# A fourth silu buffer and an earlier last product in the fast-product units of a fused attention and feed-forward kernel

## The chip, the cores and the metric

The kernel runs on one core of a Trainium2 chip. Its time is the device time of one execution in microseconds (us). The core has five instruction streams: TensorE (PE in the profile, PEld for its weight loads), VectorE (DVE), ScalarE (ACT), GpSimd (POOL) and SyncE (SP), which here only starts transfers. Each stream runs its own instructions in order and waits for the others through semaphores.

## The reference

A decaying linear attention over blocks of 64 positions (4 batches, 8 heads, 768 positions, head size 64) is followed by a gated feed-forward block on the 3072 tokens:

```python
for b in range(nb):                       # blocks of 64
    intra = einsum('bhic,bhjc->bhij', qb, kb) * Dmask
    intra = einsum('bhij,bhjd->bhid', intra, vb)
    inter = einsum('bhid,bhde->bhie', qb * lam_pow, kv_state)
    out[:, :, sl] = intra + inter
    kv_state = lam_block * kv_state + einsum('bhsd,bhse->bhde', kb * rev_pow, vb)
x = out.transpose(0, 2, 1, 3).reshape(3072, 512)
g = x @ w_gate                            # 512 x 1536
val = x @ w_val                           # 512 x 1536
return (g / (1 + exp(-g)) * val) @ w_out  # 1536 x 512
```

## The kernel before

The attention runs in twelve groups (each one batch and 256 positions). Two groups make a token tile of 512 columns, `xt`; there are six tiles, 0 to 5. While the feed-forward block of one tile runs on PE, the attention of a later tile is slipped between its products. The order of all this is written out by hand: a plan attaches pieces of attention, loads and casts to steps of tiles 0 to 3, and tiles 4 and 5 are called one after the other at the end of the body (lines 1211 to 1255). Nothing reorders instructions afterwards, so the order of the calls is each engine's order.

Tiles 0 to 3 compute gate and value products directly (`ffn_gate` L573, `ffn_val` L588): PE L581, silu on ACT L586 into a `sil` buffer, PE L599, and the product silu times value on DVE L603 into an `h` tile.

Tiles 4 and 5 use a scheme with seven block products in place of eight (Strassen's, in the Winograd form) in `ffn_unit` (L712). It is called three times for each tile (j = 0, 1, 2), each for four of the twelve column blocks of the hidden layer. The text calls these units 4/0, 4/1, 4/2 and 5/0, 5/1, 5/2. They run in the order 4/0, 4/1, output of tile 3, 4/2, 5/0, 5/1, output of tile 4, 5/2, output of tile 5. One unit has seven pairs of products on PE (all L729, eight matmuls a pair, 56 in all), pair by pair gate and value. Between them stand:

- two ACT copies of the first pair into the banks `Bb` (L763) and two of the second pair into `es` (L766);
- DVE additions `E = Bb + es` (L771) after the third pair and `es = Bb + es` (L779) after the fifth. Each reads the banks `Bb`, which a later pair of the unit overwrites: the fifth pair (weights `ws`, operand `xs`) cannot start on a bank that L771 has not read;
- four silus on ACT (L756), in the order (0,0), (1,1), (1,0), (0,1), each into a `sil` buffer, and four products silu times value (L759): three on DVE, and (1,1) on POOL, since both its operands lie in on-chip memory outside the banks;
- `drip(dr[k])` at three places: it issues up to that many pending operand sums on DVE from the list `trickle`. These are sums for the seven-product scheme: `h_combo` (L666, of h tiles for the output products), `w_combo` (L692, of weights), `x_combo` (L710, of token tiles). dr[2] is 3 in units 4/0 and 4/1 and 2 in the others;
- `mid`, in 4/0 and 4/1, which puts products of the attention of the last two groups (L514) and a short ACT copy (guard, L498) ahead of the unit's last pair.

Between 4/0 and 4/1 stand the state update of the last group, PE L420, two ACT copies `ups` of it (L442), which release two banks to 4/1's second pair, and a chain on POOL that starts from them (L475, L455, L457).

`out_units` (L801) makes a tile's output by the same scheme (all PE L819), with ACT copies (L830 and others) and DVE additions (L844, L848). Its first pair of copies, L830, must have read a bank before the next products may add to it.

Buffers come from pools: `sil` has three buffers of 1 KB a partition, also used once in the opening for `irow`; `h` has five of 6 KB; `const` holds things for the whole run, `qdec` among them. `qdec` (2 KB a partition) is the decay table of the opening: written on ACT at L209, read on DVE at L326 for the first three groups.

Of the kernel before, what the change touches and what calls it, by code (L numbers as in the profile page):

```python
# [9 lines left out]
BF16 = mybir.dt.bfloat16  # L10
# [9 lines left out]
@with_exitstack  # L20
def kernel(
    ctx: ExitStack,
    tc: tile.TileContext,
    q: bass.AP,
    k: bass.AP,
    v: bass.AP,
    lam: bass.AP,
    moe_w_gate: bass.AP,
    moe_w_val: bass.AP,
    moe_w_out: bass.AP,  # L30
    out: bass.AP,
):
    nc = tc.nc
    with tc.manual_schedule():
        _body(ctx, tc, nc, q, k, v, lam, moe_w_gate, moe_w_val, moe_w_out, out)


def _body(ctx, tc, nc, q, k, v, lam, moe_w_gate, moe_w_val, moe_w_out, out):
    B, H, S, D = q.shape
    HP = H // 2  # L40
# [8 lines left out]
    M = BLK // 2  # L49
# [12 lines left out]
    const = ctx.enter_context(tc.tile_pool(name="const", bufs=1))  # L62
# [6 lines left out]
    ssb_pool = ctx.enter_context(tc.tile_pool(name="ssb", bufs=2))  # L69
    xt_pool = ctx.enter_context(tc.tile_pool(name="xt", bufs=2))  # L70
    h_pool = ctx.enter_context(tc.tile_pool(name="h", bufs=5))
    sil_pool = ctx.enter_context(tc.tile_pool(name="sil", bufs=3))
    osb_pool = ctx.enter_context(tc.tile_pool(name="osb", bufs=4))
    kv_pool = ctx.enter_context(tc.tile_pool(name="kv", bufs=1))
    psum = ctx.enter_context(tc.tile_pool(name="psum", bufs=1, space=bass.MemoryType.PSUM))
# [121 lines left out]
    dec = const.tile([128, H, 8], FP32, name="dec")  # L197
    qdn = const.tile([128, H, 2], FP32, name="qdn")
    lamgrp = const.tile([128, HP], FP32, name="lamgrp")
    qdec = const.tile([128, HP, 2, 2 * M], BF16, name="qdec")  # L200
    nc.scalar.activation(ln_lam, lam_ps[:, 0:H], AF.Ln)
    for h2 in range(2):
        nc.scalar.activation(lnp[h2 * 64:h2 * 64 + 64, :],
# [132 lines left out]
    def run_later(n):  # L336
        for _ in range(min(n, len(later))):
            later.pop(0)()
# [312 lines left out]
    def h_combo(t, j, g=None):  # L651


        fs = slice(0, FH) if g is not None else slice(2 * j[0], 2 * j[1]) if type(j) is tuple else slice(2 * j, 2 * j + 2)
        g0, g1 = (0, B // 2) if g is None else (g, g + 1)
        ha, hb = st[("h", t, 0)], st[("h", t, 1)]
        a11, a21 = ha[:, fs, 2 * g0:2 * g1:2], ha[:, fs, 2 * g0 + 1:2 * g1:2]
        a12, a22 = hb[:, fs, 2 * g0:2 * g1:2], hb[:, fs, 2 * g0 + 1:2 * g1:2]
        for i in range(3):
            if ("hs", t, i) not in st:  # L660
                st[("hs", t, i)] = raw_pool.tile([128, FH, B // 2, BLK], BF16, name="hs", tag="raw")
        s = [st[("hs", t, i)][:, fs, g0:g1] for i in range(3)]
        for o, i0, i1, op in ((s[0], a21, a22, ALU.add), (a21, a11, a21, ALU.subtract),
                              (s[1], s[0], a11, ALU.subtract), (s[2], a12, s[1], ALU.subtract)):
            trickle.append((t, lambda o=o, i0=i0, i1=i1, op=op:
                            nc.vector.tensor_tensor(out=o, in0=i0, in1=i1, op=op)))  # L666
# [3 lines left out]
    def drip(n):  # L670
        for _ in range(min(n, len(trickle))):
            trickle.pop(0)[1]()
# [39 lines left out]
    def ffn_unit(t, j, bk, early=None, mid=None, dr=(0, 0, 2)):  # L712


        xt = st[("xt", t)]
        for half in range(2):
            if ("h", t, half) not in st:
                st[("h", t, half)] = h_pool.tile([128, FH, B, BLK], BF16, name="h", tag="h")
        hs2 = [st[("h", t, half)][:, 2 * j:2 * j + 2] for half in range(2)]
        A, E, Bb = [[banks[k] for k in bk[2 * m:2 * m + 2]] for m in range(3)]  # L720
        for k in bk:
            primed[k] = 512
        es = [kv_pool.tile([128, 2 * HP * D], FP32, name="es", tag="ups", bufs=4) for _ in range(2)]
        sil = {}

        def product(i, o, lhs, rhs, start=False):
            for fi in range(2):
                for c in range(KH):
                    nc.tensor.matmul(o[:, fi * 256:fi * 256 + 256], lhs(i, c, 2 * j + fi), rhs(c),  # L729
                                     start=(start and fi == 0 and c == 0), stop=(c == KH - 1),  # L730
                                     skip_group_check=True)

        def wa(k, half):
            def f(i, c, fc):
                f0 = (FH * half + fc) * 128
                return (wg_sb, wv_sb)[i][:, KH * k + c, f0:f0 + 128]
            return f

        def wsum(n):
            return lambda i, c, fc: ws[i, n][:, c, fc * 128:fc * 128 + 128]  # L740

        def xb(k, r):
            return lambda c: xt[:, :, KH * k + c, r]

        def xsum(n):
            return lambda c: xs[t][:, n, :, c]

        def h_of(half, r):
            return hs2[half][:, :, r:B:2]

        def v3(x):
            return x.rearrange("p (f g n) -> p f g n", f=2, g=2)

        def silu(key, src):
            sil[key] = sil_pool.tile([128, 512], BF16, name="sil", tag="sil")
            nc.scalar.activation(sil[key], src, AF.Silu)  # L756

        def mult(eng, half, r, src):
            eng.tensor_tensor(out=h_of(half, r), in0=v3(sil[half, r]), in1=v3(src), op=ALU.mult)  # L759

        for i in range(2):
            product(i, A[i], wa(0, 0), xb(0, 0), True)
            nc.scalar.copy(out=Bb[i], in_=A[i])  # L763
        for i in range(2):
            product(i, E[i], wa(0, 1), xb(0, 1), True)
            nc.scalar.copy(out=es[i], in_=E[i])  # L766
        if early:
            early()
        for i in range(2):
            product(i, Bb[i], wsum(1), xsum(1))  # L770
            nc.vector.tensor_tensor(out=E[i], in0=Bb[i], in1=es[i], op=ALU.add)  # L771
        run_later(len(later))
        drip(dr[0])
        for i in range(2):
            product(i, A[i], wa(1, 0), xb(1, 0))
        silu((0, 0), A[0])
        for i in range(2):
            product(i, Bb[i], wsum(0), xsum(0))
            nc.vector.tensor_tensor(out=es[i], in0=Bb[i], in1=es[i], op=ALU.add)  # L779
        mult(nc.vector, 0, 0, A[1])  # L780
        silu((1, 1), es[0])
        mult(nc.gpsimd, 1, 1, es[1])
        drip(dr[1])
        for i in range(2):
            product(i, E[i], wa(1, 1), xsum(2))
        silu((1, 0), E[0])
        mult(nc.vector, 1, 0, E[1])
        drip(dr[2])
        if mid:
            mid()  # L790
        for i in range(2):
            product(i, Bb[i], wsum(2), xb(1, 1))
        silu((0, 1), Bb[0])
        mult(nc.vector, 0, 1, Bb[1])
        h_combo(t, j)

    def out_row(t, b):
# [421 lines left out]
    def mid(g):  # L1219
        fixed[:] = [s0, s1]  # L1220
        core_a(g)

    trickle[:0] = [soon(w_combo, i, 3, (2, 3)) for i in range(2)]
    def early():
        fixed[:] = [s0, s1]
        scores(11)

    ffn_unit(4, 0, (aG, aV, eG, eV, bG, bV), early, lambda: mid(10), D0)
    fixed[:] = [aG, aV]
    upd_mm(11)  # L1230
# [3 lines left out]
    state(11)  # L1234
    trickle[D5:D5] = [] if XM[1] else x_soon(5, 0)
    ffn_unit(4, 1, (aG, aV, eG, eV, bG, bV), lambda: evac(10), lambda: mid(11), D1)
    core_b(11)
    drip(sum(x[0] <= 3 for x in trickle))
    trickle[:0] = x_soon(5, None if XM[1] else 1)
    out_units(3, bk=(aG, eG, bG, aV, eV, bV), many=list(M3))  # L1240
    aG, aV, eG, eV, bG, bV, s0, s1 = aG, aV, bG, bV, s0, s1, eG, eV
    ffn_unit(4, 2, (aG, aV, eG, eV, bG, bV), dr=D2)
    drip(2)
    aG, aV, eG, eV, bG, bV, s0, s1 = s0, s1, eG, eV, aG, aV, bG, bV
# [39 lines left out]
```

## Time and profile before

| | |
|---|---|
| timed runs | 218.2, 220.88, 218.67 us; median 218.67 |
| profiled execution | 217.92 us |
| its span, from first to last instruction | 216.2 us |
| busy in the span | PE 209.1, DVE 147.6, ACT 130.6, POOL 92.1 us |
| granted clock of PE in the span | 1.00 |
| ACT silu L756 waiting for POOL's product L759 | 4.7 us in 6 waits |

Rows of a timeline give the start (us from the span's start), the duration in us, the engine, the source line, the operation, what it writes and reads, the shape, and how many instructions the row merges. A bracket gives the time for which the engine stood idle just before, and what ended it. "TENSOR_TENSOR" is an operation on two tensors. A list of waits gives the waiting engine and line, what it waited for, the total in us, the number of times and the longest. PE's matmuls overlap, so a row of four matmuls that starts 0.44 us before the next can be 0.60 long.

### The profile page before, as it was taken

The numbers are of one execution on the slowest core, as the hardware profiler recorded it, in microseconds if no ns is written. First come the engines' busy times: TensorE is split into PE (matmuls) and PEld (weight loads), VectorE is DVE, ScalarE is ACT, GpSimd is POOL, SyncE is SP. The second block draws the span as 40 slices with busy tenths as digits, with TensorE's granted clock in tenths as the row PEclk, the third lists the DMA queues.
The fourth block names the chain that finished last, engine by engine and source line by source line (L and its number), as shares of the span: only waits on it lengthen the run. The fifth ranks groups of instructions, "written<-read, shape, count | busy, mean of one in ns | idle before, by whom it ended". The sixth has DMA issues, their size and how long they took to land.

```text
span 216.2 us, 6854 instructions
## 1 busy us (share of the span) xinstructions
PE 209.1 (97%) x2797; PEld 153.9 (71%) x2801; DVE 147.6 (68%) x267; ACT 130.6 (60%) x280; POOL 92.1 (43%) x128
## 2 busy tenths in 40 slices
PE   8889999899999999999999999999999999999993
PEld 3566455788888448856754545888888888888882
DVE  1774347576687889765478967887798389961750
ACT  6888576666536154548378587774882676636522
POOL 6685755828499140686953145140730022200200
PEclk9999999999999999999999999999999999999999
DMA  6999999999996788899789859763000500005014
GB/s 193 343 355 382 374 326 293 295 245 232 375 315 137 193 223 199 223 160 256 199 207 222 203 116 212 179 171 126 2 5 3 194 0 3 0 3 194 0 52 147
DMA packets 82177, 39.77 MB, mean 184 GB/s; under 512 B 45410, under 2 KB 77794, under 8 KB 82146
## 3 DMA queue, kind: packets, MB, share of 16 engines
q1 hardware_dynamic: 80946, 38.74, 65.3%
q10 hardware_dynamic: 1200, 0.59, 0.9%
q8 instruction: 22, 0.36, 0.7%
q14 instruction: 9, 0.07, 0.1%
HBM read 28.31 MB, written 6.29 MB: 160 GB/s over the span
## 4 chain that ended last, share of the span: by engine, by line
PE 89%; ACT 3%; DVE 3%; issue 1%; POOLq 1%; POOL 1%; DVEq 0%
PE bank L819 21%; PE bank L581 19%; PE bank L599 19%; PE bank L729 15%; PE bank L619 5%; PE bank L527 2%; PE bank L514 2%; DVE ssb L365 2%; PE bank L420 1%; PE bank L358 1%; PE bank L320 1%; PE bank L388 1%; PE bank L188 1%; ACT sil L756 1%; PE bank L154 1%
## 5 line engine op out<-in xcount | busy, mean ns | idle before, releaser
L603 DVE TENSOR_TENSOR h<-sil,bank 128x256 bf16<-128x256 bf16 (+1 forms) x67 | 35.1, 533 | 29.1 <-PE bank L599 17.6
L581 PE MATMUL bank<-xt,wg_sb 128*128 128x256 bf16 (+1 forms) x276 | 52.6, 315 | 0.0
L599 PE MATMUL bank<-xt,wv_sb 128*128 128x256 bf16 (+1 forms) x276 | 52.4, 314 | 0.0
L586 ACT ACTIVATE sil<-bank 128x256 bf16<-128x256 f32 (+1 forms) x67 | 31.8, 480 | 22.6 <-PE bank L581 17.6
L599 PEld LDWEIGHTS <-wv_sb 128*128 128x128 bf16 x276 | 26.9, 98 | 14.7 <-POOL wv_sb L249 0.2
L581 PEld LDWEIGHTS <-wg_sb 128*128 128x128 bf16 x276 | 26.0, 98 | 13.3 <-DVE xt L540 0.2
L266 POOL TENSOR_TENSOR v_s<-v,dec 128x512 bf16<-128x512 f32 (+1 forms) x18 | 23.2, 1308 | 25.4 <-DMA v<-in_v_dram 21.4
L759 POOL TENSOR_TENSOR h<-sil,es 128x512 bf16<-128x512 bf16 x6 | 7.0, 1167 | 47.9 <-ACT sil L756 47.9
L819 PEld LDWEIGHTS <-h 128*128 128x128 bf16 x240 | 23.3, 98 | 3.6 <-issue 0.6
L819 PE MATMUL bank<-wo_sb,h 128*128 128x256 bf16 x180 | 21.6, 273 | 0.1
L819 PEld LDWEIGHTS <-hs 128*128 128x128 bf16 x180 | 17.6, 98 | 2.7
L365 DVE TENSOR_TENSOR ssb<-bank,causal 128x512 bf16<-128x512 f32 x24 | 15.4, 683 | 2.0 <-PE bank L358 2.0
L729 PEld LDWEIGHTS <-ws 128*128 128x128 bf16 x144 | 13.8, 97 | 2.3 <-issue 0.2
L475 POOL TENSOR_TENSOR kvf<-kvs,ups 128x256 f32<-128x256 f32 x8 | 6.5, 815 | 20.5 <-ACT ups L442 20.5
L771 DVE TENSOR_TENSOR bank<-bank,es 128x512 f32<-128x512 f32 x12 | 7.8, 693 | 10.8 <-PE bank L729 9.4
L819 PE MATMUL bank<-wt,hs 128*128 128x256 bf16 x120 | 15.0, 272 | 0.0
L756 ACT ACTIVATE sil<-bank 128x512 bf16<-128x512 f32 x18 | 10.7, 596 | 7.0 <-POOL h L759 4.7
L759 DVE TENSOR_TENSOR h<-sil,bank 128x512 bf16<-128x512 bf16 x18 | 12.3, 683 | 1.5 <-ACT sil L756 1.4
L729 PE MATMUL bank<-xs,ws 128*128 128x256 bf16 x96 | 12.8, 272 | 0.0
L475 POOL TENSOR_TENSOR kvf<-kvf,ups 128x256 f32<-128x256 f32 x16 | 12.2, 764 | 0.9
L729 PE MATMUL bank<-xt,wg_sb 128*128 128x256 bf16 x72 | 10.8, 273 | 0.2 <-ACT ups L442 0.2
L619 PE MATMUL bank<-wo_sb,h 128*128 128x512 bf16 x45 | 10.7, 379 | 0.2
(119 smaller groups left out, 360.5 us busy)
## 6 DMA issues: line engine op xcount, KB each, us to landing
out_dram<-osb SPq DMA_DIRECT2D x22, 256.0 KB, 2.6
v<-in_v_dram SPq DMA_DIRECT2D x18, 256.0 KB, 4.7
woraw<-in_moe_w_out_dram SPq DMA_DIRECT2D x6, 512.0 KB, 8.2
kraw<-in_k_dram SPq DMA_DIRECT2D x24, 128.0 KB, 3.3
qraw<-in_q_dram SPq DMA_DIRECT2D x24, 128.0 KB, 3.6
wraw<-in_moe_w_gate_dram SPq DMA_DIRECT2D x5, 512.0 KB, 6.9
wraw<-in_moe_w_val_dram SPq DMA_DIRECT2D x5, 512.0 KB, 7.0
kraw<-in_k_dram SPq DMA_DIRECT2D x4, 512.0 KB, 6.7
```

The costliest lines, as they stand in the source:

```text
L266: eng.tensor_tensor(out=st[("vs", g)][:, h0:h1], in0=st[("v", g)][:, h0:h1].rearrange("p h (s d) -> p h s d", s=2), in1=vfac(g, h0, h1), o ...
L365: nc.vector.tensor_tensor(out=ssb[:, h2, 2 * c:2 * c + 2].rearrange("p a s n -> p a (s n)"), in0=sp[(c, h2)].rearrange("p (a x) -> p a x", ...
L475: nc.gpsimd.tensor_tensor(out=o, in0=f, in1=u, op=ALU.add)
L581: nc.tensor.matmul(gp[:, n0:n1], wg_sb[:, mc, fs], xt[:, g0:g1, mc].rearrange("p g b n -> p g (b n)"), start=(mc == 0 and n0 == 0), stop=( ...
L586: nc.scalar.activation(sil[:, 0:N], gp[:, 0:N], AF.Silu)
L599: nc.tensor.matmul(vp[:, n0:n1], wv_sb[:, mc, fs], xt[:, g0:g1, mc].rearrange("p g b n -> p g (b n)"), start=(mc == 0 and n0 == 0), stop=( ...
L603: nc.vector.tensor_tensor(out=h_sb[:, fc % FH, b0:b1].rearrange("p b n -> p (b n)"), in0=sil[:, 0:N], in1=vp[:, 0:N], op=ALU.mult)
L619: nc.tensor.matmul(ps, st[("h", t, fc // FH)][:, fc % FH, b], wo_sb[:, fc, c0:c1], start=(fc == 0), stop=(fc == FC - 1))
L729: nc.tensor.matmul(o[:, fi * 256:fi * 256 + 256], lhs(i, c, 2 * j + fi), rhs(c), start=(start and fi == 0 and c == 0), stop=(c == KH - 1), ...
L756: nc.scalar.activation(sil[key], src, AF.Silu)
L759: eng.tensor_tensor(out=h_of(half, r), in0=v3(sil[half, r]), in1=v3(src), op=ALU.mult)
L819: nc.tensor.matmul(o, lhs(f), rhs(f), start=(start and f == 0), stop=(f == FH - 1), skip_group_check=True)
```

## The change

One more `sil` buffer; the table `qdec` comes from the `h` pool in place of `const`; and in `ffn_unit` the third call of `drip` moves behind the last product (0,1) on DVE.

```diff
-    sil_pool = ctx.enter_context(tc.tile_pool(name="sil", bufs=3))
+    sil_pool = ctx.enter_context(tc.tile_pool(name="sil", bufs=4))
...
-    qdec = const.tile([128, HP, 2, 2 * M], BF16, name="qdec")
+    qdec = h_pool.tile([128, HP, 2, 2 * M], BF16, name="qdec", tag="h")
...
         silu((1, 0), E[0])
         mult(nc.vector, 1, 0, E[1])
-        drip(dr[2])
         if mid:
             mid()
         for i in range(2):
             product(i, Bb[i], wsum(2), xb(1, 1))
         silu((0, 1), Bb[0])
         mult(nc.vector, 0, 1, Bb[1])
+        drip(dr[2])
         h_combo(t, j)
```

## The prediction

> **What bounds the kernel now.** I read the page first, then the list of waits, then the timeline of the last third, where the changed function runs. The page:
>
> ```profile
> span 216.2 us, 6854 instructions
> ...
> PE 89%; ACT 3%; DVE 3%; issue 1%; POOLq 1%; POOL 1%; DVEq 0%
> ```
>
> The chain that ended last runs through TensorE (PE) for 89% of the span. Another engine matters only where it makes PE late, so the question is which PE delays the two edits can touch. The list of waits names the candidate:
>
> ```profile
> ACT sil L586 <- PE bank L581: 17.6, 33, 1.1
> ...
> ACT sil L756 <- POOL h L759: 4.7, 6, 0.8
> ```
>
> Six times, once in each unit of tiles 4 and 5, ScalarE (ACT) stands still some 0.8 us before a silu until GpSimd (POOL) has finished its product h(1,1). A unit makes four silus in the order (0,0), (1,1), (1,0), (0,1). In the built program the fourth gets the buffer of the second, (1,1), whose reader is that POOL product: hence the wait. (Columns: total us, times, longest.) The 4.7 us are ACT time, not PE time. What PE loses is read from the starts of its units:
>
> ```profile
> 168.71 0.60 PE L729 MATMUL bank<-xt,wg_sb 128*128 128x256 bf16 x4
> ...
> 172.21 1.04 PE L729 MATMUL bank<-xs,ws 128*128 128x256 bf16 x8
> ...
> 174.82 0.60 PE L729 MATMUL bank<-xt,wg_sb 128*128 128x256 bf16 x4
> ...
> 181.23 0.60 PE L729 MATMUL bank<-xt,wg_sb 128*128 128x256 bf16 x4
> ...
> 187.53 2.67 PE L819 MATMUL bank<-wo_sb,h 128*128 128x256 bf16 x23
> ```
>
> The third unit of tile 4 (call it 4/2) takes 174.82 - 168.71 = 6.11 us for 56 matmuls, 0.109 us each: PE at its own pace. Unit 5/0 takes 6.41 and 5/1 takes 6.30. So 0.30 and 0.19 us are lost there. Two more losses stand in the timeline, at the seam of 4/0 and 4/1 and behind 5/2; their rows follow.
>
> **Buffers and the table.** The decay table takes the first h buffer. The h tiles move one place on among the five buffers, and in the built program no product that writes one gets a wait that it did not have. The table's last reader (L326) belongs to tile 0's stage, and the buffer is needed again only in tile 2. I cost it at nothing; were that cover gone, one VectorE (DVE) product would wait. The fourth silu buffer moves each silu's wait one reader back. In the built program's order, ACT, POOL, PE and SP issue the same instructions in the same sequence; no DMA moves in any queue. The only order that changes is DVE's, in four units (4/0, 4/1, 5/0, 5/1), and the silu (0,1) no longer names POOL. In tiles 0 to 3 I cost the fourth buffer at nothing: a silu there waits for its PE product in 33 cases and PE runs through. No row shows a gain or a loss there, so I keep ±0.1 us.
>
> **Step 1, the seam of 4/0 and 4/1.**
>
> ```profile
> 150.70 1.35 DVE L759 TENSOR_TENSOR h<-sil,bank 128x512 bf16<-128x512 bf16 x2
> ...
> 150.92 1.17 POOL L759 TENSOR_TENSOR h<-sil,es 128x512 bf16<-128x512 bf16 x1 [8.04 <-ACT sil L756]
> ...
> 151.36 0.39 PE L420 MATMUL bank<-v_s,qk 64*64 64x64 bf16 x18
> ...
> 151.97 0.42 DVE L692 TENSOR_TENSOR wg_sb<-wg_sb 128x512 bf16<-128x512 bf16 x1
> ...
> 152.13 0.60 ACT L756 ACTIVATE sil<-bank 128x512 bf16<-128x512 f32 x1 [0.75 <-POOL h L759]
> ...
> 152.30 0.42 DVE L692 TENSOR_TENSOR wv_sb<-wv_sb 128x512 bf16<-128x512 bf16 x1
> ...
> 152.47 0.60 PE L729 MATMUL bank<-xt,wv_sb 128*128 128x256 bf16 x4
> ...
> 152.62 0.86 ACT L442 COPY ups<-bank 128x512 f32<-128x512 f32 x2
> ...
> 153.25 0.60 PE L729 MATMUL bank<-xt,wg_sb 128*128 128x256 bf16 x4 [0.18 <-ACT ups L442]
> 153.28 0.72 POOL L475 TENSOR_TENSOR kvf<-kvs,ups 128x256 f32<-128x256 f32 x1 [1.18 <-ACT ups L442]
> ...
> 154.07 0.85 POOL L455 CAST kvn<-kvf 64x256 bf16<-64x256 f32 x2
> ...
> 154.99 1.30 DVE L771 TENSOR_TENSOR bank<-bank,es 128x512 f32<-128x512 f32 x2 [1.34 <-ACT es L766]
> 155.00 0.73 POOL L475 TENSOR_TENSOR kvf<-kvf,ups 128x256 f32<-128x256 f32 x1
> ...
> 155.87 1.07 PE L729 MATMUL bank<-xs,ws 128*128 128x256 bf16 x8
> ```
>
> The third group of matmuls should follow the second after 4 x 0.109, at 152.91; it came at 153.25, 0.34 late, released by the first copy of L442. That copy stood behind the silu that waited 0.75 for POOL. Without the wait the silu runs from 151.38 (152.13 - 0.75) to 151.98, and the copy begins near 151.93 instead of 152.62: its PE input L420, from 151.36 on, is through by then, as PE's next unit starts at 152.03 (152.47 - 0.44). Its release, 0.63 after its start as now, comes at 152.56, ahead of 152.91: the 0.34 is gone.
>
> What is late next? POOL's L475 follows the same copy by 0.66 and now starts at 152.59. The edit puts the product (0,1) first on DVE, from 152.05 (150.70 + 1.35) to 152.73, and the three sums (two L692, one L666), which ran from 151.97 on, come behind it: beside L475 and L455, which before ran after them. What such a meeting costs is shown earlier in the trace:
>
> ```profile
> 77.46 2.46 POOL L266 TENSOR_TENSOR v_s<-v,dec 128x1024 bf16<-128x1024 f32 x1 [6.45 <-DMA v<-in_v_dram]
> ...
> 78.07 2.27 DVE L666 TENSOR_TENSOR hs<-h 128x768 bf16<-128x768 bf16 x1
> ...
> 80.38 0.56 DVE L666 TENSOR_TENSOR h<-h 128x768 bf16<-128x768 bf16 x1
> ```
>
> A sum that takes 0.56 alone took 2.27 and ended 0.42 after POOL did (80.34 against 79.92): it was held until POOL was through, and then needed its own time less 0.14. For our sums of 0.42 that is 0.28 after POOL's end. If the two engines take turns: L475 to 153.32, first sum to 153.60, half of L455 (0.43) to 154.03, second sum to 154.31, the other half to 154.74, third sum to 155.02. L771 then starts at about 154.95 (0.09 before the end of its forerunner, as 152.30 stands to 151.97 + 0.42). It stands at 154.99 now, waiting for the ACT copy L766, which also moves up. PE's product at 155.87 overwrites the banks that L771 reads; its second half (0.44 later) waits for L771's end, 154.95 + 1.30 = 156.25, against 156.29 now. So PE arrives 0.34 earlier and waits 0.30 longer: worth 0.04, and POOL's chain, 0.69 earlier and held three times 0.28 less its own short gaps, ends as before. I take 0.0. Bounds: 0.37 gained if nothing is held (0.34, and the 0.03 by which 1.07 at 155.87 exceeds the 1.04 of unit 4/2), 0.9 lost under the third rival.
>
> The Trainium skill, page SBUF — State Buffer, section "SBUF: two separate sides", says that a DVE instruction with two SBUF inputs and a GpSimd instruction that reads SBUF lock each other out of one port pair for the whole instruction. By that rule the three sums are held as above; without it the step would give 0.37 instead of 0.0. The 2.27 us row agrees with it.
>
> **Step 2, units 5/0 and 5/1.**
>
> ```profile
> 172.84 1.29 DVE L779 TENSOR_TENSOR es<-bank,es 128x512 f32<-128x512 f32 x2 [0.38 <-PE bank L729]
> ...
> 175.48 0.60 ACT L756 ACTIVATE sil<-bank 128x512 bf16<-128x512 f32 x1 [0.80 <-POOL h L759]
> ...
> 177.71 1.29 DVE L771 TENSOR_TENSOR bank<-bank,es 128x512 f32<-128x512 f32 x2
> ...
> 179.09 1.29 DVE L779 TENSOR_TENSOR es<-bank,es 128x512 f32<-128x512 f32 x2
> ...
> 180.29 1.42 DVE L759 TENSOR_TENSOR h<-sil,bank 128x512 bf16<-128x512 bf16 x2
> ...
> 181.62 0.42 DVE L666 TENSOR_TENSOR hs<-hs,h 128x512 bf16<-128x512 bf16 x1
> ...
> 182.42 0.68 DVE L759 TENSOR_TENSOR h<-sil,bank 128x512 bf16<-128x512 bf16 x1
> ...
> 183.21 0.42 DVE L666 TENSOR_TENSOR hs<-h 128x512 bf16<-128x512 bf16 x1
> ...
> 184.01 1.29 DVE L771 TENSOR_TENSOR bank<-bank,es 128x512 f32<-128x512 f32 x2
> ...
> 184.82 1.13 PE L729 MATMUL bank<-xs,ws 128*128 128x256 bf16 x8
> ```
>
> In 5/0 the late silu of 4/2 (0.80) delays the ACT copies and, through product (0,1) and two sums, L771. All of these move up by more than the 0.30 that PE lost, so 5/0 falls to 6.11 and 5/1 starts at 180.93.
>
> In 5/1 the limit is another one. DVE has no gap from 177.71 to 184.01: 6.30 us of its own work per unit, against 6.11 of PE's. L779 of 5/0 can start no earlier than its PE product, 4.13 after the unit's start as in 4/2 (172.84 - 168.71): 178.95, only 0.14 earlier. From there: 1.20 to the products (180.29 - 179.09), three of them at 0.67 (half of 181.62 - 180.29), four sums in two pairs of 0.80 (182.42 - 181.62, 184.01 - 183.21): 178.95 + 1.20 + 2.00 + 1.60 = 183.75 for L771, 0.26 earlier than now. Here the new order itself saves 0.12, the difference between 0.79 (182.42 to 183.21, a sum that waits for the product just ahead) and 0.67. L771 ends at 185.04. PE's second half of the product wants those banks at 180.93 + 3.50 (172.21 - 168.71) + 0.44 = 184.87 and waits 0.2. Before, that half went at 184.01 + 1.29 = 185.30. So the two units together return 0.26 of their 0.49. Ends: 0.14 (only L779's shift) and 0.49.
>
> **Step 3, the seam behind 5/2.**
>
> ```profile
> 203.46 0.60 ACT L756 ACTIVATE sil<-bank 128x512 bf16<-128x512 f32 x1 [0.79 <-POOL h L759]
> ...
> 203.96 0.78 ACT L830 COPY bank<-bank 128x256 f32<-128x256 f32 x2
> ...
> 204.39 2.50 PEld L819 LDWEIGHTS <-h 128*128 128x128 bf16 x23 [0.27 <-issue]
> ```
>
> PE's weight loads stop for 0.27 until the first L830 copy, held behind the same silu, has read a bank. With the silu 0.79 earlier the copy starts as its product ends, some 0.25 earlier, and ends just as PE wants the bank. I take 0.25 (0.20 to 0.27); behind it PE and the last stores run as now.
>
> **Sum.** 0.0 + 0.26 + 0.25 = 0.5 us. The profiled execution took 217.92 (span 216.2 and 1.7 around it), below the median 218.67 of the timed runs (218.2, 218.67, 220.88). The median of all four is 218.4, so I forecast 217.9; against the profile's own time it would be 217.4.
>
> **Rivals.** (a) Nothing is held in step 1: DVE's sums slip between POOL's. For it: DVE's first L692 at 151.97 overlapped POOL's product by 0.12 at no cost. Against: the 2.27 row. It gives 0.37 + 0.26 + 0.25 = 0.9, so 217.5. (b) The change does nothing measurable: the freed ACT time is covered by DVE, which is full in tile 5, and each seam finds its next wait. For it: step 1 as I cost it, and DVE without a gap from 177.71. Against: 204.39, where no DVE work stands between. 218.4. (c) Slower: POOL keeps the port from L475 through L455 to the next L475, 2.45 us (155.00 + 0.73 - 153.28) from 152.59 to 155.04, and all three sums follow, 0.28 and twice 0.33: L771 starts near 155.9, 0.9 later than now, PE waits with it, and the 0.5 saved elsewhere leaves +0.4: 218.8. It decides from an L771 later than 155.5. Against: in the quoted rows POOL too gives way (2.46 where the sum came in).
>
> **How the numbers follow.** My forecast 0.5, (a) 0.2, (b) 0.17, (c) 0.11, and 0.02 for something not seen. The range runs from 216.8 (the profile's 217.92 less all 1.1 of lost PE time: 0.34, 0.30, 0.19, 0.27) to 219.2 (the timed median plus (c)). Every named case lies within 2% of 218.67 (4.4 us, about what a measurement of this kernel can tell from no change), so same holds 0.96; 0.01 is left for faster and 0.03 for slower.
>
> **What would show it.** The wait of ACT L756 for POOL L759 is gone. L442 starts near 151.9, but L771 of 4/1 still near 155.0 and a sum L692 or L666 there lasts over 0.6 us. Units 5/0 and 5/1 take 6.11 and about 6.3 us, in 5/1 PE waiting for L771. The 0.27 behind 5/2 falls below 0.1. Wrong would be PE gaps in tiles 0 to 3 that were not there, L771 of 4/1 before 154.7 (case a) or behind 155.5 (case c), or a 5/1 at 6.11.

## The result and the profile after

The changed kernel took 217.06 us (median of 16 runs, 216.62 to 218.59) against 218.76 for the kernel before on the same chip (16 runs, 217.87 to 221.37): a ratio of 0.9931 with a 95% interval of 0.9907 to 0.9956, which is 1.5 us (the medians are 1.7 apart). Run again later beside other kernels (`e7`), the same kernel gave a ratio of 0.9953 (0.9927 to 0.9978), 1.0 us. The forecast was 217.9, a gain of 0.5. The profiled execution after took 216.62 us (before: 217.92). The page after, in the lines that answer to those of before:

```profile
span 214.9 us, 6858 instructions
...
PE 92%; DMA 2%; DVE 1%; SPq 1%; ACT 0%; issue 0%; DVEq 0%
```

The span is 1.3 us shorter. ACT and POOL have all but left the chain that ended last (they had 3% and 1%), and the group "ACT sil L756 <- POOL h L759", 4.7 us before, is gone from the list of waits.

Where the time went is read best from the starts of PE's groups, stage by stage. The table gives the distances in us between PE rows of the profiled executions of all kernels of this study. "Enters" is the first matmul of L514 in unit 4/0. "To 4/2" runs from there to the start of 4/2 and holds the seam of 4/0 and 4/1. "Behind" runs from the start of 5/2 to the last output product, and holds the seam behind 5/2. The two stages left out, 4/2 (6.11) and the output of tile 4 (9.17), differ by more than 0.01 in one kernel only (9.25 in `e4`).

| kernel | enters | to 4/2 | 5/0 | 5/1 | behind | all |
|---|---|---|---|---|---|---|
| before | 149.98 | 18.73 | 6.41 | 6.30 | 14.33 | 61.05 |
| after | 149.76 | 18.31 | 6.11 | 6.21 | 14.08 | 59.99 |
| after, run again (`e7`) | 150.83 | 18.30 | 6.11 | 6.20 | 14.08 | 59.98 |
| `e1` buffer and table, old order | 150.22 | 19.07 | 6.12 | 6.40 | 14.07 | 60.94 |
| `e2` new order alone | 149.93 | 18.96 | 6.40 | 6.88 | 14.32 | 61.85 |
| `e3` table alone | 151.61 | 18.73 | 6.40 | 6.30 | 14.33 | 61.04 |
| `e9` as `e1`, the three sums of 4/0 moved into 4/1 | 149.90 | 18.30 | 6.12 | 6.40 | 14.08 | 60.18 |
| `e5` after, five sums for three | 152.44 | 19.62 | 6.11 | 6.21 | 14.07 | 61.29 |
| `e10` after, one cast for two halves | 151.24 | 18.55 | 6.11 | 6.21 | 14.08 | 60.23 |
| `e11` after, four quarter casts | 150.24 | 18.73 | 6.11 | 6.21 | 14.08 | 60.42 |
| `e4` after, sums of tile 5 later | 150.64 | 18.30 | 6.12 | 6.11 | 14.08 | 59.97 |
| `e8` after, sums of tile 5 later still | 151.22 | 18.30 | 6.11 | 6.12 | 14.07 | 59.88 |

The change is worth 1.06 us from unit 4/0 on: 0.42 at the first seam, 0.30 and 0.09 in units 5/0 and 5/1, 0.25 behind 5/2. Its second profile gives 1.07. What lies ahead of unit 4/0 differs by 1.07 us between two profiles of one and the same kernel (149.76 and 150.83), so the 0.22 between before and after in that column proves nothing. A row of each shows where the difference begins: an ACT cast of the opening that waits for its transfer, 0.87 us before, 0.17 after, 1.54 in the repeat.

```profile
37.12 1.04 ACT L289 CAST qk<-kraw 128x1024 bf16<-128x1024 f32 x1 [0.87 <-DMA kraw<-in_k_dram]
```

```profile
36.43 1.04 ACT L289 CAST qk<-kraw 128x1024 bf16<-128x1024 f32 x1 [0.17 <-DMA kraw<-in_k_dram]
```

```profile
37.95 1.04 ACT L289 CAST qk<-kraw 128x1024 bf16<-128x1024 f32 x1 [1.54 <-DMA kraw<-in_k_dram]
```

The 1.06 of the table lies inside the intervals of both timed gains, 1.5 and 1.0 us.

The seam of 4/0 and 4/1 in the timeline after. This execution is 0.21 us ahead of the one before on entering it, so 0.21 is added to a start to set it beside the rows of before:

```profile
150.48 1.95 DVE L759 TENSOR_TENSOR h<-sil,bank 128x512 bf16<-128x512 bf16 x3
...
151.05 0.61 ACT L756 ACTIVATE sil<-bank 128x512 bf16<-128x512 f32 x1
...
151.67 0.86 ACT L442 COPY ups<-bank 128x512 f32<-128x512 f32 x2
...
152.33 0.72 POOL L475 TENSOR_TENSOR kvf<-kvs,ups 128x256 f32<-128x256 f32 x1 [0.46 <-ACT ups L442]
152.35 0.98 DVE L692 TENSOR_TENSOR wg_sb<-wg_sb 128x512 bf16<-128x512 bf16 x1
152.69 0.60 PE L729 MATMUL bank<-xt,wg_sb 128*128 128x256 bf16 x4
...
153.12 1.01 POOL L455 CAST kvn<-kvf 64x256 bf16<-64x256 f32 x2
...
153.26 0.61 DVE L692 TENSOR_TENSOR wv_sb<-wv_sb 128x512 bf16<-128x512 bf16 x1
...
153.79 0.62 DVE L666 TENSOR_TENSOR h<-h 128x512 bf16<-128x512 bf16 x1
...
154.39 1.30 DVE L771 TENSOR_TENSOR bank<-bank,es 128x512 f32<-128x512 f32 x2
```

The silu has no wait in its bracket any more, and the first copy of L442 follows it at once; PE's group at 152.69 follows its forerunner (152.26) after 0.43, its own pace. The three sums last 0.98, 0.61 and 0.62 us where they took 0.42 each: they are held. But L771 starts at 154.39, 154.60 on the clock of before, not at the 154.95 of the prediction, and that is early enough for PE.

A second path at this seam got shorter too. POOL's chain ends in the casts of the state that PE's products L514 of unit 4/1 read. Before, these products took 0.44 us up to the unit's last pair (157.74 to 158.18); now they take 0.38 (157.15 to 157.53). The rows before, then the row after:

```profile
156.94 0.85 POOL L455 CAST kvn<-kvf 64x256 bf16<-64x256 f32 x2
...
157.75 0.30 PE L514 MATMUL bank<-qkt,kvn 64*64 64x64 bf16 x5
```

```profile
157.17 0.24 PE L514 MATMUL bank<-qkt,kvn 64*64 64x64 bf16 x5
```

Before, the second cast ended at 157.79, after the products had begun; now the casts end at 157.06, 157.27 on the clock of before, and the products run through. No bracket names this short wait, but `e11` below lengthens the same path and shows it.

Units 5/0 and 5/1 after:

```profile
174.18 0.60 PE L729 MATMUL bank<-xt,wg_sb 128*128 128x256 bf16 x4
...
180.29 0.60 PE L729 MATMUL bank<-xt,wg_sb 128*128 128x256 bf16 x4
...
182.98 1.29 DVE L771 TENSOR_TENSOR bank<-bank,es 128x512 f32<-128x512 f32 x2
...
183.79 1.13 PE L729 MATMUL bank<-xs,ws 128*128 128x256 bf16 x8
...
186.50 2.78 PE L819 MATMUL bank<-wo_sb,h 128*128 128x256 bf16 x24
```

5/0 runs at PE's pace (6.11), 5/1 takes 6.21; the group at 183.79 lasts 1.13 in place of 1.04, since its second half waits for L771, which ends at 184.27. Behind 5/2 the weight loads run through without the 0.27 gap, and the next products follow after 205.72 - 201.79 = 3.93 us, the pace of 36 matmuls at 0.109:

```profile
201.68 3.92 PEld L819 LDWEIGHTS <-h 128*128 128x128 bf16 x36
201.79 4.10 PE L819 MATMUL bank<-wo_sb,h 128*128 128x256 bf16 x36
202.70 0.36 ACT L830 COPY bank<-bank 128x256 f32<-128x256 f32 x1 [0.49 <-PE bank L819]
...
205.72 2.88 PE L819 MATMUL bank<-wt,hs 128*128 128x256 bf16 x24
```

### The profile page after: what moved, and what is told of

It is laid out like the page before. It is cut to its first block, busy times and chain, and to the rows that moved or that the text cites. A ratio compares the mean times of both kernels' runs of the same rounds, so it can differ in the third digit from the quotient of the medians.

```text
span 214.9 us, 6858 instructions
## 1 busy us (share of the span) xinstructions
PE 208.0 (97%) x2797; PEld 153.4 (71%) x2801; DVE 147.9 (69%) x267; ACT 131.1 (61%) x280; POOL 92.2 (43%) x128
## 4 chain that ended last, share of the span: by engine, by line
PE 92%; DMA 2%; DVE 1%; SPq 1%; ACT 0%; issue 0%; DVEq 0%
PE bank L819 22%; PE bank L581 20%; PE bank L599 19%; PE bank L729 17%; PE bank L619 5%; PE bank L527 3%; DMA kraw<-in_k_dram 2%; PE bank L514 2%; PE bank L420 2%; PE bank L358 1%; DVE ssb L365 1%; SPq L115 1%; PE bank L388 1%; PE bank L320 1%; ACT qk L304 0%
## 5 line engine op out<-in xcount | busy, mean ns | idle before, releaser
L759 POOL TENSOR_TENSOR h<-sil,es 128x512 bf16<-128x512 bf16 x6 | 7.0, 1164 | 47.4 <-ACT sil L756 47.4
L475 POOL TENSOR_TENSOR kvf<-kvs,ups 128x256 f32<-128x256 f32 x8 | 6.5, 815 | 19.3 <-ACT ups L442 19.3
L771 DVE TENSOR_TENSOR bank<-bank,es 128x512 f32<-128x512 f32 x12 | 7.8, 694 | 9.6 <-PE bank L729 9.6
L756 ACT ACTIVATE sil<-bank 128x512 bf16<-128x512 f32 x18 | 10.5, 596 | 3.7 <-PE bank L729 3.7
L475 POOL TENSOR_TENSOR kvf<-kvf,ups 128x256 f32<-128x256 f32 x16 | 12.3, 766 | 0.9
L759 DVE TENSOR_TENSOR h<-sil,bank 128x512 bf16<-128x512 bf16 x18 | 11.8, 683 | 0.3 <-ACT sil L756 0.3
```

What stands on the lines that cost most here:

```text
L475: nc.gpsimd.tensor_tensor(out=o, in0=f, in1=u, op=ALU.add)
```

## The experiments

Each expectation names its own theories; "theory A" is the one held when that run was written. The first was that the silu's wait for POOL's product is the whole cost, so that the fourth buffer brings the gain and the order of the sums is a detail. A diff shows the lines that matter, with cuts marked by dots. `e1` to `e4` ran on one chip (before: 218.34 us), `e5`, `e7`, `e8` and `e9` on one (before: 218.61), `e10` and `e11` on one (a single timed run each, beside one of before: 218.31).

**The buffer and the table, with the old order (`e1`).**

```diff
         mult(nc.vector, 1, 0, E[1])
+        drip(dr[2])
         if mid:
...
         mult(nc.vector, 0, 1, Bb[1])
-        drip(dr[2])
```

> Fourth silu buffer and the table in an h buffer, the sums left ahead of the last product. Theory A (the gain is PE time lost behind the silu that waits for POOL): ACT L756 no longer waits for POOL L759; the 0.34 us at the seam of 4/0 and 4/1, the 0.30 us in 5/0 and the 0.27 us behind 5/2 are gone; 5/1 keeps a loss of some 0.2 us, because there DVE is the limit and a sum right behind the product it reads costs 0.12 more. Together 0.9 to 1.1 us below the kernel before, ratio about 0.9955. Rival B (the gain comes from the product moved ahead of the sums): no change, ratio 1.000, and PE losses as before.

Measured 218.41 us, ratio 1.0007 (0.9982 to 1.0032). The theory missed. Rival B had the number but not the reason: it let PE's losses stay as before, and two of them are gone. The table shows 5/0 and the last seam gaining as in the changed kernel, and the seam of 4/0 and 4/1 losing 0.34 where the changed kernel gains 0.42. Its timeline there:

```profile
152.79 0.76 POOL L475 TENSOR_TENSOR kvf<-kvs,ups 128x256 f32<-128x256 f32 x1 [0.46 <-ACT ups L442]
152.88 0.95 DVE L666 TENSOR_TENSOR h<-h 128x512 bf16<-128x512 bf16 x1
...
153.76 0.68 DVE L759 TENSOR_TENSOR h<-sil,bank 128x512 bf16<-128x512 bf16 x1
...
154.52 0.57 ACT L763 COPY bank<-bank 128x512 f32<-128x512 f32 x1 [0.70 <-DVE h L759]
...
155.14 0.60 PE L729 MATMUL bank<-xs,ws 128*128 128x256 bf16 x4 [0.52 <-ACT bank L763]
```

The freed silu lets L442 and with it POOL's L475 start earlier, and now they meet the third sum, which goes ahead of the product (0,1) on DVE. The sum takes 0.95 us in place of 0.42. Behind it stands the product, behind the product the copy L763 that overwrites the bank the product reads, and behind the copy PE. In 5/1 the old order costs 0.19 against the new one (6.40 to 6.21), since the product and L771 come later.

**The new order alone (`e2`), and the table alone (`e3`).** `e2` goes back to three `sil` buffers and to `qdec` in `const` (the diff is against the changed kernel); `e3` goes back to three buffers (the first pair of these lines) and to the old order (the diff of `e1`).

```diff
-    sil_pool = ctx.enter_context(tc.tile_pool(name="sil", bufs=4))
+    sil_pool = ctx.enter_context(tc.tile_pool(name="sil", bufs=3))
...
-    qdec = h_pool.tile([128, HP, 2, 2 * M], BF16, name="qdec", tag="h")
+    qdec = const.tile([128, HP, 2, 2 * M], BF16, name="qdec")
```

> Three silu buffers and the table as before, the last product ahead of the sums. Theory A: slower. DVE now stands still until the silu that waits for POOL is through (about 0.7 us in 4/0, 4/1, 5/0 and 5/1), and the sums come later by that much; L771 of 5/1, where DVE has no slack, comes 0.5 to 0.7 us later and PE waits with it; at the seam of 4/0 and 4/1 L771 is 0.3 us late. Together 0.5 to 1.1 us above the kernel before, ratio 1.002 to 1.005. Rival B: faster by 0.5 us or more, ratio 0.998 or below.

Measured 219.24 us, ratio 1.0047 (1.0018 to 1.0077): slower by half a percent, as theory A had it, and by the table 0.80 us from unit 4/0 on, most of it (0.58) in 5/1. The timeline there:

```profile
182.57 0.69 DVE L759 TENSOR_TENSOR h<-sil,bank 128x512 bf16<-128x512 bf16 x1 [0.69 <-ACT sil L756]
...
184.76 1.29 DVE L771 TENSOR_TENSOR bank<-bank,es 128x512 f32<-128x512 f32 x2
...
185.51 1.20 PE L729 MATMUL bank<-xs,ws 128*128 128x256 bf16 x8 [0.36 <-DVE bank L771]
```

With three buffers the silu still waits for POOL; DVE now stands idle for it 0.69 us, which the sums had filled, and they follow behind.

> Only the decay table in an h buffer. Theory A: no change, ratio 0.999 to 1.001, PE losses in tiles 4 and 5 as before (6.41 and 6.30 us for 5/0 and 5/1), and PE's start of tile 1's first step (39.17 us before, 38.81 us in the changed kernel) anywhere between, since it hangs on a transfer. Rival C (the table's place gave the 0.2 to 0.36 us found in the opening): that step starts near 38.8 us and the time is 0.2 to 0.4 us lower, ratio 0.9985.

Measured 218.69 us, ratio 1.0023 (0.9998 to 1.0048). Every stage of the table is that of before. The table's move does nothing measurable by itself. (No run has the fourth buffer with the table left in `const`.) So the two halves of the change give -0.11 and +0.80 alone and -1.06 together.

**Is it the sums at that seam? (`e9`, and `e5` from the other side).** `e9` is `e1` with the third `drip` of unit 4/0 empty; its three sums run in unit 4/1 behind L771.

```diff
-    D0 = (0, 0, 3)
+    D0 = (0, 0, 0)
```

> Fourth silu buffer and table, the sums ahead of the last product as in the kernel before, but none of them in unit 4/0 (its three go to the end of 4/1). Theory A (with the buffer alone the seam lost time because POOL's L475 held the third sum, and with it the last product and the copy L763 that waits for it): the last product follows its silu, L763 does not wait for DVE, the seam gains the 0.43 us that the changed kernel gained, 5/0 0.29, the seam behind 5/2 0.25, 5/1 loses 0.1: 0.85 us below the kernel before from tile 4 on, ratio 0.996. If the seam's loss had another cause, the copy L763 still waits and the sum stays near 0.1.

Measured 216.91 us, ratio 0.9932 (0.9908 to 0.9955): with the old order and without the sums the seam gains 0.43, all of it. The timed gain, 1.5 us (1.0 to 2.0), is larger than the table's 0.87; the table holds nothing from ahead of unit 4/0, and what the rest is stays open. L771 starts 4.64 us after the first L514 of 4/0 (after: 154.39 - 149.76 = 4.63), and not DVE but ACT sets it:

```profile
154.54 1.30 DVE L771 TENSOR_TENSOR bank<-bank,es 128x512 f32<-128x512 f32 x2 [1.97 <-ACT es L766]
```

So three held sums fill just the 1.97 us for which L771 would wait anyway. `e5` is the changed kernel with two more sums there:

```diff
-    D0 = (0, 0, 3)
+    D0 = (0, 0, 5)
```

> The changed kernel with five sums in place of three behind the last product of unit 4/0, ahead of L771 of unit 4/1. Theory A (POOL's seam chain holds DVE's sums, and L771 there has under 0.1 us to spare): the two extra sums meet POOL's L475 and L457 and last over 0.6 us each, L771 comes 1.2 us later (154.39 to about 155.6), PE waits some 1.1 us in 4/1, and the whole is 0.6 to 1.1 us above the changed kernel. If the sums are not held they take 0.4 each, L771 comes 0.8 later. If L771 does not bound PE there, PE's times stay as in the changed kernel.

Measured 218.97 us, ratio 1.002 (0.999 to 1.005). The seam loses 1.31 against the changed kernel:

```profile
157.01 0.94 DVE L666 TENSOR_TENSOR hs<-hs,h 128x512 bf16<-128x512 bf16 x1
...
158.41 1.28 DVE L771 TENSOR_TENSOR bank<-bank,es 128x512 f32<-128x512 f32 x2
...
159.15 1.20 PE L729 MATMUL bank<-xs,ws 128*128 128x256 bf16 x8 [0.99 <-DVE bank L771]
```

Theory A forecast this path and a loss of some 1.1 us. So the path by which the prediction wanted to charge step 1 is real: sums held, L771 late (5.97 after the first L514), PE waiting for it. Three sums were too few for it here, five were enough.

**For how long does a POOL instruction hold a sum? (`e10`, `e11`).** In the changed kernel L455 casts a part of the last group's state in two halves of 64 partitions, which it swaps. `e10` casts it in one piece and leaves out the swap, so that its state is not the reference's; `e11` casts it in four pieces.

```diff
-        if g >= NAT0 and n % 2 == 0:
+        if g >= NAT0 and n % 2 == 0 and g < 11:
```

> The changed kernel with the casts L455 of the last group made whole: one cast of 128x256 (alone 0.40 us) in place of two of 64x256, so POOL has 0.4 us less work beside the three sums (the halves are not swapped, so the last group's state is left out of order). Theory A: DVE and POOL take turns instruction by instruction, so one POOL instruction less ahead of the third sum puts that sum beside the second L475 (0.72 alone). The sums then last about 0.98, 0.61 and 0.94 us in place of 0.98, 0.61 and 0.62, L771 of 4/1 starts 4.96 us after tile 4/0's first L514 (4.63 in the changed kernel), and PE loses some 0.3 us in 4/1. Rival: what counts is the POOL work ahead of L771; less of it makes the sums shorter or leaves them (at most 0.98, 0.61, 0.62), L771 at 4.63 or earlier, and PE loses nothing.

```profile
154.59 0.47 POOL L457 CAST kvn<-kvf 128x256 bf16<-128x256 f32 x1
...
154.73 0.61 DVE L692 TENSOR_TENSOR wv_sb<-wv_sb 128x512 bf16<-128x512 bf16 x1
155.03 0.90 POOL L475 TENSOR_TENSOR kvf<-kvf,ups 128x256 f32<-128x256 f32 x1
...
155.27 0.95 DVE L666 TENSOR_TENSOR h<-h 128x512 bf16<-128x512 bf16 x1
...
156.14 1.28 DVE L771 TENSOR_TENSOR bank<-bank,es 128x512 f32<-128x512 f32 x2
...
156.88 1.19 PE L729 MATMUL bank<-xs,ws 128*128 128x256 bf16 x8
```

The sums last 0.98, 0.61, 0.95; L771 starts 4.90 after the first L514 and PE loses 0.24 (theory A: 4.96 and 0.3; the one timed run took 218.42). One POOL instruction less made DVE later: the third sum now meets the long L475. The two take turns, and the order of POOL's instructions decides.

```diff
-            for h2 in range(2):
...
+            cs = (0, HP) if g < 11 else (0, HP // 2, HP)
+            for h2, c in [(h2, c) for h2 in range(2) for c in range(len(cs) - 1)]:
...
```

> The changed kernel with each half cast L455 of the last group cut in two (64x128, four casts in place of two). Theory A: the second and the third sum each wait for one quarter cast; what a cast holds the port for grows with its size, so the sums last about 0.98, 0.5 and 0.5 us (0.61 and 0.62 with the halves, 0.42 alone). Rival: a turn has a fixed price, whatever the size of POOL's instruction: 0.98, 0.61, 0.62 again. By both PE gains nothing in 4/1, since L771 starts no earlier than the ACT copy L766 allows, 4.6 us after the first L514.

```profile
153.59 1.47 POOL L456 CAST kvn<-kvf 64x128 bf16<-64x128 f32 x4
153.73 0.51 DVE L694 TENSOR_TENSOR wv_sb<-wv_sb 128x512 bf16<-128x512 bf16 x1
154.16 0.51 DVE L668 TENSOR_TENSOR h<-h 128x512 bf16<-128x512 bf16 x1
154.86 1.30 DVE L773 TENSOR_TENSOR bank<-bank,es 128x512 f32<-128x512 f32 x2 [0.20 <-ACT es L768]
...
157.08 1.09 POOL L456 CAST kvn<-kvf 64x128 bf16<-64x128 f32 x4
...
157.99 0.10 PEld L516 LDWEIGHTS <-kvn 64*64 64x64 bf16 x1 [0.22 <-POOL kvn L456]
```

(Lines are 1 or 2 further here; the one timed run took 217.52.) The second and the third sum last 0.51: against 0.42 alone, a cast of 128 elements a partition costs a sum 0.09 us, one of 256 elements 0.19 or 0.20 (0.61, 0.62), on 64 or on 128 partitions (`e10`) alike. So the price grows with the elements, and a turn has no fixed price.

The ends of the rows say it more simply. In `after`, `e1`, `e4`, `e5`, `e10` and `e11` each held sum ends 0.28 us after the POOL instruction that it met, whichever that was (in `e10`, for example, 154.73 + 0.61 = 155.34 against 154.59 + 0.47 = 155.06). And the POOL instruction ends 0.15 us after the end of the sum ahead of it where it is a cast of 128 elements, 0.25 or 0.26 where it is one of 256, and 0.59 where it is L475 (in `e10`, 155.93 against 155.34).

That PE loses nothing, as both theories said, was wrong: it lost 0.43, on another path. The eight quarter casts make POOL's chain 0.63 longer (its end 7.93 after the first L514 of 4/0 in place of 7.30), and the state comes too late for the L514 of unit 4/1. In the changed kernel the chain ends, at 157.06, only 0.09 us before these products begin:

```profile
156.21 0.85 POOL L455 CAST kvn<-kvf 64x256 bf16<-64x256 f32 x2
...
157.15 0.10 PEld L514 LDWEIGHTS <-kv 64*64 64x64 bf16 x1 [0.21 <-issue]
```

**What is left in tile 5 (`e4`, `e8`), and the repeat (`e7`).** `e4` runs the two sums that stood between 5/0 and 5/1 in the middle of 5/1. `e8` runs them at its end, and holds back the sums at the first two places in the output of tile 4; its diff also takes out the `drip(2)`.

```diff
-    drip(2)
...
-    ffn_unit(t, 1, (aG, aV, eG, eV, bG, bV))
+    ffn_unit(t, 1, (aG, aV, eG, eV, bG, bV), dr=(0, 2, 2))
```

> The changed kernel with two sums of unit 5/0 moved from ahead of L771 of unit 5/1 to behind its first product, so that DVE has 0.8 us less to do between L779 of 5/0 and L771 of 5/1. Theory A: 5/1 falls from 6.21 to 6.11 us, L771 there waits for PE and PE for nothing, and the whole is 0.1 us below the changed kernel, ratio to the kernel before about 0.993. If DVE is not what limits 5/1, it stays at 6.21 us.

Measured 217.56 us, ratio 0.9966 (0.9938 to 0.9993). 5/1 falls to 6.11: DVE's load was its limit. But a moved sum now runs beside POOL's product h(1,1) and is held (1.07 in place of 0.42), and the output of tile 4 gets 0.08 longer, so that of the 0.1 us expected 0.02 is left:

```profile
186.73 1.16 POOL L759 TENSOR_TENSOR h<-sil,es 128x512 bf16<-128x512 bf16 x1 [4.95 <-ACT sil L756]
187.10 1.07 DVE L666 TENSOR_TENSOR hs<-h 128x512 bf16<-128x512 bf16 x1
```

```diff
+    ffn_unit(t, 1, (aG, aV, eG, eV, bG, bV), dr=(0, 0, 4))
...
-    out_units(t - 1, bk=(s0, aG, bG, s1, eG, aV), many=[2])
+    out_units(t - 1, bk=(s0, aG, bG, s1, eG, aV), many=[0, 0])
```

> The changed kernel with the sums of unit 5/0 moved behind the last product of 5/1 and those of 5/1 behind the first addition (L844) of the output of tile 4. Theory A: L771 of 5/1 waits for PE and 5/1 takes 6.11 us; no sum stands beside a POOL product, and the output of tile 4 takes 9.17 us as before. PE needs 1.16 us less from tile 4 on than in the kernel before, 0.1 less than in the changed kernel; ratio 0.9945. If DVE is full in the output of tile 4 as well, that takes 0.1 us longer.

> The changed kernel as it is, once more, beside the others on one chip. From tile 4 on PE's losses are as in its first profile (5/0 6.11, 5/1 6.21 us, no gap at the two seams), 1.07 us below the kernel before; ratio 0.995. If the 0.2 us that its first profile gained ahead of tile 4 belongs to the change, PE enters tile 4 at 143.95 us again; if it hangs on transfers, anywhere from 143.9 to 145.8.

Measured for `e8` 217.73 us, ratio 0.9946 (0.9921 to 0.9971), for `e7` on the same chip 217.27, 0.9953 (0.9927 to 0.9978). In the trace `e8` is the shortest from unit 4/0 on, 0.11 below the changed kernel, and nothing of the PE losses that the prediction listed is left in it. In the time the two can't be told apart.

## Why the prediction was right in kind and short in size

- **Buffers and the table, nothing.** Held for everything from unit 4/0 on (`e3`: all stages as before). For tiles 0 to 3 the ±0.1 stays open: two executions of the changed kernel come to unit 4/0's L514 1.07 us apart.
- **Step 1, 0.0 forecast, 0.42 measured.** This is the step that failed, in one term that it used twice. PE's 0.34 came back as worked out; L442 starts at 151.88 on the clock of before (151.93 forecast); the order of turns was right, and so was the 0.28 by which a sum ends after the POOL instruction that it meets (153.33 against 153.05 for the first). The failing term is "half of L455 (0.43)": I took a cast's start-to-start time as the time from the end of one sum to the end of the cast behind it. The two halves end at 153.59 and 154.13, only 0.25 and 0.26 after the sum ahead of each: the first starts at 153.12, while that sum still runs. So each of the next two sums ended 0.54 us after the one before, not 0.71 (0.43 + 0.28), and the third 0.40 earlier than forecast. L771 came 0.35 earlier; by then not the sums alone set it, since it starts 0.03 after the end of the first copy L766 (154.36), just as before (154.96 and 154.99). The same term let POOL's chain end "as before"; it ended 0.5 earlier, which gave PE the 0.06 at L514. The 0.34, this 0.06 and the 0.03 that PE had lost at L771 make up the 0.42 within rounding, more than the bound of 0.37 that the prediction set for nothing held. `e11` shows the price as one of elements; `e5` and `e10` show that the rest of the argument holds as soon as the sums need longer. The Trainium skill, page SBUF — State Buffer, section "SBUF: two separate sides", speaks of a lock for the whole instruction: the traces agree that a sum waits until the POOL instruction is through, and POOL's in turn, but with 0.43 as the length of the cast a turn would be 0.71, where 0.54 was measured.
- **Step 2, 0.26 forecast, 0.39 measured.** 5/0 fell to 6.11 as worked out, and L779 starts 4.13 after the unit's start, as forecast. From there to L771 the forecast was 4.80 us, measured 182.98 - 178.31 = 4.67: the three products in a row took 1.87 in place of 2.00. I had priced each by half of a pair of before (1.33), and in that pair the second product starts only at 181.02, 0.73 after the first, as its silu had just ended (180.99). The sums, 1.59 for 1.60, were right. DVE is still the limit of 5/1 (`e4`, `e8`).
- **Step 3, 0.25 forecast, 0.25 measured.**
- **Sum and rivals.** 0.5 forecast, 1.06 measured from unit 4/0 on. The time, 217.06, lies in the range of 216.8 to 219.2, but that range held every rival too, so it speaks for none of them. Rival (a), nothing held, gave 0.9 and was nearest in size, and its mark, L771 before 154.7, was met at 154.60, which the prediction had named as a sign of being wrong. Rival (a)'s reason was wrong as well, since all three sums are held: its 0.9 was near by luck. Rival (c) did not come, but `e5` shows its late L771 with PE waiting, without POOL keeping DVE out throughout; rival (b)'s seam that finds its next wait is that of `e1`. Neither the prediction nor its rivals saw that the buffer without the new order is worth next to nothing: I costed the new order as a loss at the seam (sums beside POOL) and a gain of 0.12 in 5/1, and didn't ask what the old order would meet once the wait is gone.

## What to carry to other kernels

When a wait is removed, look at what the same engine's neighbours now meet: here the freed ACT copy brought POOL forward onto DVE's sums, and only sums placed behind the product, on whose end the next copy hangs, left PE alone. Price a meeting of DVE and POOL by a measured meeting of the same kind, not by the POOL instruction's own duration. And compare stage by stage from a common point: what lies ahead of unit 4/0 moved by as much as the whole change.

## What the runs showed of the hardware

- A DVE sum of two on-chip operands (0.42 us alone) that meets a POOL instruction ends 0.28 us after that instruction does, be it a cast, the addition L475 or the product L759 (`after`, `e1`, `e4`, `e5`, `e10`, `e11`). Beside a cast it lasts 0.61 with 256 elements a partition and 0.51 with 128; beside L475 0.94 to 0.98; beside the product of 512 elements (1.16 us) 1.07. One that started later behind the sum ahead lasted 0.50 beside a cast of 256 (`e5`). The number of partitions, 64 or 128, made no difference (`e10`).
- POOL gives way too: L475, 0.72 alone, takes 0.90 between two sums (`e10`), and the two half casts 1.01 in place of 0.85.
- In turns, a POOL instruction ends 0.15 us after the sum ahead of it (cast of 128 elements, `e11`), 0.25 or 0.26 (cast of 256, `after`) or 0.59 (L475, `e10`).
- POOL's state chain ends 0.09 us before PE's products that read it begin; a chain 0.63 us longer (`e11`) cost PE 0.43.
